# Small VectorE operations split or moved to other forms, transposes planned at their traced length, last feed-forward slots given earlier due numbers

## The chip, the cores and the metric

One core of one Trainium2 chip. The time is the device time of the whole kernel in microseconds: the median of several runs. The engines are named as in the profile: PE (TensorE matmul), PEld (TensorE weight load), DVE (VectorE), ACT (ScalarE), POOL (GpSimd), SP (the queue that issues most DMAs).

## The reference, cut to what matters

```python
# q, k, v: (4, 8, 576, 64); x below: 2304 tokens of 512
scores = q @ k.T / 8
kth    = 32nd largest of each row
attn   = softmax(where(scores >= kth, scores, -1e9)) @ v
h = x @ w_in                                  # 512 -> 2048
x = where(h > 0, h, exp(min(h, 0)) - 1) @ w_out   # 2048 -> 512
logits = normed(x) @ normed(expert_emb).T / tau   # 8 experts
e, gate = argmax(logits), softmax(logits)[e]
out = gate * (relu(x @ w1[e]) @ w2[e])        # 512 -> 1024 -> 512
```

## The kernel before, in words

The kernel has two stages. The first computes attention, the feed-forward layer and the routing, token slot by token slot; the second runs the eight experts on the tokens gathered for each.

Attention works on 144 tiles, each 128 query rows by 576 keys. Two tiles (the two heads of a pair) share one score buffer in SBUF (`arena`), one mask buffer and one transpose. `tile_ops` (from line 760) makes a tile's steps and `threshold` (line 663) its search for the 32nd largest score: PE computes the scores in two halves (L783), ACT copies them to SBUF (L789), VectorE takes the best eight of seven pieces (L677) and from these the best 24 (L687, L689), then a threshold (L691), ACT takes signs against it (L692), VectorE masks the row (L705; in the first 20 tiles POOL does, L703), appends a nine-column filler (L707), finds the next eight (L709) and the final bound (L710). Line 698 makes the exponent's bias from the row maximum, once for each pair of tiles, as three columns read sixteen apart, of which two are used. After that ACT makes a mask (L808), POOL subtracts it (L816), ACT takes the exponential (L818), POOL splits it into two f16 parts (L821, L825), SP transposes these by DMA (L827), and PE multiplies by v (L857). After every eighth tile VectorE counts for a proof that the threshold was right (L715, L716, 8 tiles each).

Keys are fetched by `get_k` (line 533): transposed on PE into the PSUM tile `misc`, of which there is one buffer, and cut into three bf16 parts. For the first 512 columns `thirds` (line 521) does that with ACT copies (L524) and PE matmuls that subtract in PSUM (L526). For the last 64 columns VectorE subtracts (L569, L571) between two ACT copies (L568, L570). Values are cut in two f16 parts by `get_v`: ACT the first (L593), VectorE the second (L597), one instruction for each head.

When the tiles of a slot of 128 tokens are done, `norm_ops` scales the sum (L889), splits it (L894, L895) and transposes it by DMA (L904). `ffn_ops` (line 908) runs the feed-forward layer of the slot in four units of 512 hidden columns: PE (L916 to L918) into the one buffer `hp`, ACT (L938, L939), VectorE (L940), ACT or POOL (L945, L943), POOL (L946), PE (L923 to L925) into `y`. There are 18 slots, counted from 0. `route_ops` (line 957) copies `y` (L962), computes the eight logits of each token (L970, L999), the best expert and its one-hot row (L1000 to L1003), the rank of the token in its expert (L974, L975, L1007, L1008), and the gate (L1006). After slot 14, `first_tokens` gathers 128 tokens of expert 0 (L1026, L1027).

The order on every engine is fixed when the kernel is built. Each step is handed to a planner with an engine, a cost in ns and a due number; the planner (`Plan.emit`, line 149) walks through planned time and starts, of the steps that are ready on an engine, the one with the smallest due number. Due numbers count tiles: a step due at `n` belongs beside tile `n`. Engines then execute their lists in order; a step that waits holds up all behind it on its engine. The costs are numbers in the code: 62 for line 698, 480 for line 1003, 2000 or 1360 for the transposes on SP.

Of the kernel before, what the change touches and what calls it, by code (L numbers as in the profile page):

```python
# [24 lines left out]
BLK = 8  # L25
# [164 lines left out]
def topk_attention_ffn_experts_kernel(  # L190
# [156 lines left out]
    def attention_and_ffn(fast):  # L347
# [185 lines left out]
        def get_k(b, p, due):  # L533
# [15 lines left out]
            def trl():  # L549
                nc.tensor.transpose(m2.t[:, 0:SL], x.t[1].rearrange("p h d -> p (h d)"), ident[0:64, 0:64])  # L550
# [207 lines left out]
        pair, all_s, all_h = {}, [], []  # L758

        def tile_ops(n):  # L760
# [30 lines left out]
            if fast:  # L791
                both = threshold(n, sb, sb.t, top, k, kb, h, sc, halves)
# [700 lines left out]
```

## Time and profile before

| | |
|---|---|
| median of 3 runs | 1298.32 us (1296.48 to 1306.35) |
| profiled execution | 1295.57 us |
| its span, first to last instruction | 1293.7 us |
| busy share of the span | PE 80%, PEld 61%, DVE 71%, ACT 65%, POOL 60% |
| mean granted clock of TensorE | 0.899 of full |

A busy share is an average over both stages. The windows split the span by time; the groups give the mean duration of each instruction of one line and form; a timeline row gives start and duration. An instruction's duration is from its start to its end on the engine; short ones overlap the next by up to some 0.07 us. A duration includes the time in which the engine stands inside the instruction, unable to go on.

### The profile page before, as it was taken

How to read it: one execution, taken by the hardware profiler on the slowest of the kernel's cores; microseconds unless marked ns; L12 is line 12 of the kernel's file. 1: busy time of each engine (PE TensorE's matmuls, PEld its weight loads, DVE VectorE, ACT ScalarE, POOL GpSimd, SP SyncE). 2: the span in 40 equal slices, each digit the busy share in tenths (PEclk: the TensorE clock that was granted, in tenths of full speed). 3: DMA queues.
4: the chain of work that ended last, by engine and by line, in shares of the span. 5: the costliest groups of instructions: out<-in, count | busy, mean ns of one | idle time of the engine just before them, and what ended most of it. 6: DMA issues, size and time to landing. Idle time of an engine off the chain costs nothing. (4 is left out here: it accounts for less than half of the span.)

```text
span 1293.7 us, 28474 instructions
## 1 busy us (share of the span) xinstructions
PE 1037.9 (80%) x10047; PEld 795.6 (61%) x10048; DVE 922.7 (71%) x3597; ACT 846.7 (65%) x1791; POOL 777.0 (60%) x816
## 2 busy tenths in 40 slices
PE   3465446899778899898889978898897779998996
PEld 2344335677556676666566656676664568887885
DVE  4889999798889899999988978998411345334410
ACT  3577768788777788887778958887531345444421
POOL 2258679787778788678878758897622233333300
PEclk9666666899799999899999979998988889999998
DMA  7985642556873558845475655553523555555400
GB/s 207 298 221 141 169 113 50 110 95 142 162 135 61 111 103 150 176 86 99 90 133 101 136 117 103 106 87 68 140 53 91 197 179 180 184 180 167 148 18 17
DMA packets 321732, 165.85 MB, mean 128 GB/s; under 512 B 257990, under 2 KB 298054, under 8 KB 321552
## 3 DMA queue, kind: packets, MB, share of 16 engines
q1 hardware_dynamic: 316816, 150.67, 51.6%
q0 software_dynamic: 4736, 12.92, 3.3%
q8 instruction: 95, 1.56, 0.5%
q14 instruction: 85, 0.70, 0.2%
HBM read 77.43 MB, written 11.40 MB: 69 GB/s over the span
## 5 line engine op out<-in xcount | busy, mean ns | idle before, releaser
L916 PE MATMUL hp<-xt,ww 128*128 128x128 f16 x1152 | 218.2, 230 | 21.3 <-DVE rr L940 20.5
L816 POOL TENSOR_TENSOR arena<-arena,k 128x576 f32<-128x576 f32 x144 | 189.2, 1316 | 76.1 <-ACT k L808 73.7
L917 PE MATMUL hp<-xt,ww 128*128 128x128 f16 x1152 | 217.9, 229 | 0.0
L918 PE MATMUL hp<-xt,ww 128*128 128x128 f16 x1152 | 217.5, 229 | 0.0
L825 POOL TENSOR_TENSOR php<-arena,php 128x576 f16<-128x576 f32 x144 | 187.3, 1301 | 5.8
L783 PE MATMUL sc<-arena_r,qd 128*128 128x288 bf16 (+1 forms) x960 | 149.5, 315 | 50.4 <-DMA arena_r<-big 18.7
L677 DVE MAX8 cand<-arena 128x8 f32<-128x82 f32 (+1 forms) x1008 | 160.9, 228 | 32.1 <-ACT arena L789 31.6
L789 ACT ACTIVATE arena<-sc 128x288 f32<-128x288 f32 x288 | 112.6, 406 | 76.6 <-PE sc L783 72.9
L857 PEld LDWEIGHTS <-pt 128*128 128x128 f16 (+3 forms) x2400 | 100.7, 105 | 99.0 <-DMA pt<-php 55.6
L783 PEld LDWEIGHTS <-qd 128*128 128x128 bf16 (+1 forms) x960 | 87.5, 108 | 96.0 <-issue 37.3
L857 PE MATMUL acc<-vb,pt 128*128 128x64 f16 (+1 forms) x1920 | 93.1, 202 | 56.7 <-DMA pt<-php 44.9
L916 PEld LDWEIGHTS <-ww 128*128 128x128 f16 x1152 | 119.7, 104 | 25.2 <-DVE rr L940 13.8
L821 POOL TENSOR_SCALAR php<-arena 128x576 f16<-128x576 f32 x144 | 101.6, 706 | 55.7 <-ACT arena L818 54.4
L692 ACT ACTIVATE k<-arena,mba 128x576 bf16<-128x576 f32 x144 | 111.6, 775 | 32.0 <-DVE mba L691 26.1
L917 PEld LDWEIGHTS <-ww 128*128 128x128 f16 x1152 | 119.2, 103 | 17.9 <-issue 11.8
L808 ACT ACTIVATE k<-arena,mba 128x576 bf16<-128x576 f32 x144 | 111.7, 775 | 19.3 <-DVE mba L710 14.2
L918 PEld LDWEIGHTS <-ww 128*128 128x128 f16 x1152 | 119.5, 104 | 0.0
L818 ACT ACTIVATE arena<-arena,mx 128x576 f32<-128x576 f32 x144 | 111.5, 775 | 11.4 <-POOL arena L816 9.4
L925 PE MATMUL y<-ww,gt 128*128 128x512 f16 x288 | 111.0, 385 | 3.1 <-POOL gt L946 3.1
L923 PE MATMUL y<-ww,gt 128*128 128x512 f16 x288 | 112.0, 389 | 1.6 <-ACT big L962 1.0
L709 DVE MAX8 w<-w 128x8 f32<-128x585 f32 x144 | 109.8, 762 | 4.0 <-POOL w L703 2.9
L924 PE MATMUL y<-ww,gt 128*128 128x512 f16 x288 | 111.2, 386 | 0.0
(303 smaller groups left out, 2774.9 us busy)
## 6 DMA issues: line engine op xcount, KB each, us to landing
arena<-in_moe_w_dram SPq DMA_DIRECT2D x52, 512.0 KB
arena_r<-big SPq DMA_DIRECT2D x64, 144.0 KB
big<-in_moe_w_out_dram SPq DMA_DIRECT2D x16, 512.0 KB
ww<-in_moe_w_in_dram SPq DMA_DIRECT2D x14, 512.0 KB
qd<-big SPq DMA_DIRECT2D x32, 192.0 KB
ysc<-big SPq DMA_DIRECT2D x20, 258.0 KB
w<-in_moe_w_dram SPq DMA_DIRECT2D x10, 512.0 KB
big<-in_v_dram SPq DMA_DIRECT2D x9, 512.0 KB
```

Source lines behind the costliest of these rows:

```text
L677: v.max(out=cand.t[:, 8 * g:8 * g + 8], in_=x()[:, ENDS[g]:ENDS[g + 1]])
L692: op("act", 760, n + K["dsg"], lambda: nc.scalar.activation(k.t(), x(), AF.Sign, scale=-1.0, bias=th.t, accum_out=ds.t), r=[sb, th, k.base ...
L783: nc.tensor.matmul(o[64 * g:64 * g + 64] if s is None else o, qd.t[:, i, g, p * n:p * n + n], kt.t[:, g, i // 2, cs], start=i == 0, stop=i ...
L789: op("act", 291, n - K["dcp"], lambda c=c: nc.scalar.activation(sb.t()[:, c * 288:c * 288 + 288], sc.t[:, SC0 + c * 288:SC0 + c * 288 + 28 ...
L808: op("act", 667, n + K["drl"], lambda: nc.scalar.activation(k.t(), sb.t(), AF.Relu, scale=-HUGE, bias=kb.t), r=[sb, kb, s2, k2], w=[k])
L816: op("pool", 1242, e, lambda sb_=sb_, k_=k_: nc.gpsimd.tensor_tensor(sb_.t(), sb_.t(), k_.t(), op=ALU.subtract), r=[k_, s2, k2], w=[sb_])
L825: op("pool", 1270, e + K["dlo"], lambda sb_=sb_, i=i: nc.gpsimd.tensor_tensor(ph.t[:, i, 1, 0:S], sb_.t(), ph.t[:, i, 0, 0:S], op=ALU.subt ...
L857: nc.tensor.matmul(acc.t[out_, cs], t[h][rows, g, :], rhs, start=(i == 0), stop=(i == len(units) - 1))
L916: nc.tensor.matmul(hp.t[:, i * 128:i * 128 + 128], wi_at(0, kb, fb), xh, start=(kb == 0), stop=False)
L917: nc.tensor.matmul(hp.t[:, i * 128:i * 128 + 128], wi_at(0, kb, fb), xl, start=False, stop=False)
L918: nc.tensor.matmul(hp.t[:, i * 128:i * 128 + 128], wi_at(1, kb, fb), xh, start=False, stop=(kb == KB - 1))
L923: nc.tensor.matmul(y.t, gt.t[:, 0, i, :], wo_at(0, fb), start=(fb == 0), stop=False)
```

## The change

The diff makes these edits (lines of the kernel before):

1. The bias of the exponential (L698): instead of one instruction of three columns for each pair of tiles, one of a single column for each tile (144 instead of 64 with three columns and 16 with one).
2. The last 64 columns of a key block go through `thirds` like the first 512: three ACT copies from PSUM and two PE matmuls, and no VectorE step.
3. The second part of the values (L597): one VectorE instruction for both heads.
4. The proof counts (L715, L716) are made after every 16th tile.
5. Routing: the logits are written to a spare part of `misc` in PSUM and read from there by L1000, L1001 and ACT's L1006; the rank sum (L1007) goes to PSUM too and is read there by L1008. The one-hot row (L1003) is written as nine columns, three by three, from a new constant `rev9`, whose rows of three are four apart.
6. The planner's cost of the transpose on SP: 3100 and 1900 instead of 2000 and 1360. Other costs follow edits 1 to 5.
7. The last four feed-forward slots (14, 15, 16, 17) get due numbers 1, 2, 3 and 4 tiles earlier at their first unit and twice as much earlier at their end.

```diff
-BLK = 8
+BLK = 16
...
+    rev9 = const.tile([128, 3, 4], F32, name="rev9")
+    for i in range(9):
+        nc.vector.memset(rev9[:, i // 3, i % 3:i % 3 + 1], float(E - i))
...
-            mx = None
-            if h or tiles[n][3] is None:
-
-                mx = r_mx()
-                op("dve", 62, n + .3, lambda: v.tensor_scalar(mx.t[:, 0:2 * h + 1], top.t[:, 0:32 * h + 1:16], -scale, None, op0=ALU.mult), r=[top], w=[mx])
+            if not h:
+                pair["mx"] = r_mx()
+            mx2, mx = pair["mx"], Buf(t=1)
+            op("dve", 62, n + .3, lambda: v.tensor_scalar(mx2.t[:, h:h + 1], place(0)[:, 0:1], -scale, None, op0=ALU.mult), r=[top, mx2], w=[mx])
...
-            left = r_left()
-            end = piece(SM, SL)
-            op("act", 110, due - U, lambda: nc.scalar.activation(end(0), m2.t[:, 0:SL], AF.Copy), r=[m2, kn], w=[kx2])
-            op("dve", 130, due - U, lambda: nc.vector.tensor_tensor(left.t, m2.t[:, 0:SL], end(0), op=ALU.subtract), r=[m2, kn, kx2], w=[left])
-            op("act", 110, due - U, lambda: nc.scalar.activation(end(1), left.t, AF.Copy), r=[left, kn], w=[kx2])
-            op("dve", 130, due - U, lambda: nc.vector.tensor_tensor(end(2), left.t, end(1), op=ALU.subtract), r=[left, kn], w=[kx2])
+            thirds(kx2, m2, SL, due - U, piece(SM, SL), 110, [kn])
...
-                for hd in range(2):
-                    op("dve", 700 if i == 0 else 300, due, lambda i=i, hd=hd: lo(i, hd), r=[x, b_sv], w=[d])
+                op("dve", 950 if i == 0 else 400, due, lambda i=i: lo(i), r=[x, b_sv], w=[d])
...
-            op("sp", 2000 if nh == 2 else 1360, e + .6, lambda: nc.sync.dma_start_transpose(
+            op("sp", 3100 if nh == 2 else 1900, e + .6, lambda: nc.sync.dma_start_transpose(
...
+            def LG():
+                return m2.t[:, 3 * E:4 * E]
...
-            op("dve", 380, e, lambda: v.scalar_tensor_tensor(X(1)[:, 2], X(1)[:, 0], X(1)[:, 1, 0:1], rev8, op0=ALU.is_equal, op1=ALU.mult), r=[x, lgt, mx], w=[er])
+            op("dve", 130, e, lambda: v.scalar_tensor_tensor(X(1)[:, 2], LG(), X(1)[:, 1, 0:1], rev8, op0=ALU.is_equal, op1=ALU.mult), r=[x, m2, lgt, mx], w=[er])
...
-            op("dve", 480, e, lambda: v.tensor_scalar(X(2), rev8, X(1)[:, 3, 0:1], None, op0=ALU.is_equal), r=[x, er], w=[one_])
+            op("dve", 130, e, lambda: v.tensor_scalar(
+                X(2).rearrange("p (a b) -> p a b", a=3), rev9[:, :, 0:3], X(1)[:, 3, 0:1], None, op0=ALU.is_equal), r=[x, er], w=[one_])
...
-            op("act", 290, e, lambda: nc.scalar.activation(X(1)[:, 4], X(1)[:, 0], AF.Exp, bias=X(0)[:, 2:3], accum_out=X(0)[:, 3:4]), r=[x, lgt, ng], w=[pr])
+            op("act", 290, e, lambda: nc.scalar.activation(X(1)[:, 4], LG(), AF.Exp, bias=X(0)[:, 2:3], accum_out=X(0)[:, 3:4]), r=[x, m2, lgt, ng], w=[pr])
...
-                ffn_ops(where[b, j], e, e + K["ffd"])
+
+                c = max(0, where[b, j] - NSLOT + 5)
+                ffn_ops(where[b, j], e - c, e - c + K["ffd"] - c)
```

What that does to the order, at three places. The line numbers of the changed kernel differ: between 680 and 810 they are one or two lower (its 686, 690, 696, 703, 705, 707, 708, 713, 714, 787 and 806 are 687, 691, 698, 705, 707, 709, 710, 715, 716, 789 and 808 of before), its 527 is 524 (and 568, 570), its 591 is 593, its 1001 to 1006 are 998 to 1003, its 1011 to 1016 are 1007 to 1012; from 818 to 962 they are the same.

VectorE at the threshold of the last tile, before:

```order
2096 L687 MAX top<-cand 128x8
2097 L691 TENSOR_SCALAR mba<-top 128x1
2098 L698 TENSOR_SCALAR mx<-top 128x3
2099 L705 SCALAR_TENSOR_TENSOR w<-sc,mba,arena 128x576
2100 L707 TENSOR_SCALAR w<-ramp,dsa 128x9
2101 L709 MAX w_14209<-w 128x8
2102 L710 TENSOR_SCALAR mba<-w_14209 128x1
2103 L715 TENSOR_TENSOR ge<-w_14209,mba 128x64
```

and now:

```order
2120 L686 MAX top<-cand 128x8
2121 L690 TENSOR_SCALAR mba<-top 128x1
2122 L696 TENSOR_SCALAR mx<-top 128x1
2123 L703 SCALAR_TENSOR_TENSOR w<-sc,mba,arena 128x576
2124 L705 TENSOR_SCALAR w<-ramp,dsa 128x9
2125 L707 MAX w_13445<-w 128x8
2126 L708 TENSOR_SCALAR mba<-w_13445 128x1
2127 L713 TENSOR_TENSOR ge<-w_13445,mba 128x128
2128 L714 TENSOR_REDUCE cnta<-ge 128x16
```

The three-column instruction is now one of a single column, and the count covers sixteen tiles.

VectorE from the scaling of the last slot (L889) on, with the feed-forward step L940 (one for each unit) and the routing of slot 16, before:

```order
2125 L889 TENSOR_TENSOR rr<-acc,rinv 128x512
2126 L1012 RECIPROCAL big<-ss 128x1
2127 L1007 TENSOR_TENSOR L<-misc,bcap 128x8
2128 L1008 SCALAR_TENSOR_TENSOR L,ss<-L,oh 128x8
2129 L1010 TENSOR_TENSOR bcap<-misc,bcap 128x8
2130 L940 SCALAR_TENSOR_TENSOR rr<-hp,sc_115,rr 128x512 x3
2131 L998 RECIPROCAL ss<-ss 128x1
2132 L999 TENSOR_SCALAR L<-misc,ss,taub 128x8
2133 L1000 MAX L<-L 128x8
2134 L1001 SCALAR_TENSOR_TENSOR L<-L,rev_81 128x8
2135 L1002 MAX L<-L 128x8
2136 L1003 TENSOR_SCALAR oh<-rev_81,L 128x8
```

and now:

```order
2154 L889 TENSOR_TENSOR rr<-acc,rinv 128x512
2155 L1001 RECIPROCAL ss<-ss 128x1
2156 L1002 TENSOR_SCALAR misc<-misc,ss,taub 128x8
2157 L1003 MAX L<-misc 128x8
2158 L1004 SCALAR_TENSOR_TENSOR L<-misc,L,rev_81 128x8
2159 L1005 MAX L<-L 128x8
2160 L1006 TENSOR_SCALAR oh<-rev_83,L 128x9
2161 L1011 TENSOR_TENSOR misc<-misc,bcap 128x8
2162 L1012 SCALAR_TENSOR_TENSOR L,ss<-misc,oh 128x8
2163 L1014 TENSOR_TENSOR bcap<-misc,bcap 128x8
2164 L1016 RECIPROCAL big<-ss 128x1
2165 L940 SCALAR_TENSOR_TENSOR rr<-hp,sc_125,rr 128x512 x4
```

Before, two units of slot 16 stood behind L889 (in the x3, with one of slot 17); now all four of slot 17 and none of slot 16, and slot 16's routing is finished ahead of slot 17's first unit.

ACT at the third key block of the second batch, whose last 64 columns are the rows with 128x64, before:

```order
622 L524 ACTIVATE big<-misc 128x512
623 L593 ACTIVATE vb<-vraw,sv 128x8x64
624 L789 ACTIVATE arena<-sc 128x288
625 L568 ACTIVATE big<-misc 128x64
626 L808 ACTIVATE k<-arena,mba 128x576
627 L789 ACTIVATE arena<-sc 128x288
628 L570 ACTIVATE big<-left 128x64
```

and now:

```order
636 L527 ACTIVATE big<-misc 128x512
637 L939 ACTIVATE rr<-rr,sc_125 128x512
638 L591 ACTIVATE vbl<-vrawl,sv 64x2x64
639 L527 ACTIVATE big<-misc 128x64
640 L806 ACTIVATE k<-arena,mba 128x576
641 L787 ACTIVATE arena<-sc 128x288
642 L527 ACTIVATE big<-misc 128x64
643 L787 ACTIVATE arena<-sc 128x288 x3
644 L527 ACTIVATE big<-misc 128x64
```

There are three copies out of `misc` instead of one out of `misc` and one out of `left`, with other steps of ACT between them.

## Rows read from the trace of the kernel before

**Rows 1.** Windows: length, busy PE, PEld, DVE, ACT, POOL, clock, DMA share, GB/s.

```profile
0.00:100.00 100.00, 47.99 (x308) 33.95 (x310) 68.21 (x259) 58.58 (x125) 32.46 (x35) 0.72 0.86 242
...
100.00:200.00 100.00, 45.69 (x435) 35.09 (x434) 98.33 (x299) 72.56 (x137) 74.67 (x54) 0.62 0.50 131
...
200.00:900.00 700.00, 605.91 (x6956) 448.52 (x6957) 626.93 (x2777) 564.63 (x1277) 545.73 (x608) 0.94 0.59 111
```

**Rows 2.** VectorE instruction groups by form: total busy, mean ns, idle before.

```profile
L709 DVE MAX8 w<-w 128x8 f32<-128x585 f32 x144 | 109.8, 762 | 4.0 <-POOL w L703 2.9
...
L687 DVE MAX8 top<-cand 128x8 f32<-128x56 f32 x432 | 85.2, 209 | 2.4
...
L698 DVE TENSOR_SCALAR mx<-top 128x3 f32<-128x3 f32 x64 | 44.8, 699 | 0.0
...
L707 DVE TENSOR_SCALAR w<-ramp,dsa 128x9 f32<-128x9 f32 x144 | 30.5, 212 | 10.6 <-ACT k L692 10.0
...
L597 DVE SCALAR_TENSOR_TENSOR vb<-vraw,sv,vb 128x256 f16<-128x256 f32 x32 | 24.3, 759 | 2.0 <-ACT vb L593 1.9
...
L691 DVE TENSOR_SCALAR mba<-top 128x1 f32<-128x1 f32 x144 | 20.9, 145 | 1.4
...
L597 DVE SCALAR_TENSOR_TENSOR vbl<-vrawl,sv,vbl 64x64 f16<-64x64 f32 x32 | 18.8, 588 | 2.5 <-ACT vbl L593 2.5
...
L571 DVE TENSOR_TENSOR big<-left,big 128x64 bf16<-128x64 f32 x16 | 13.1, 816 | 2.7 <-ACT big L570 2.6
...
L715 DVE TENSOR_TENSOR ge<-w,mba 128x64 f32<-128x64 f32 x18 | 12.8, 713 | 0.0
...
L1003 DVE TENSOR_SCALAR oh<-rev,L 128x8 bf16<-128x8 f32 x18 | 9.8, 542 | 0.1
...
L1001 DVE SCALAR_TENSOR_TENSOR L<-L,rev 128x8 f32<-128x8 f32 x18 | 9.3, 514 | 0.1
...
L569 DVE TENSOR_TENSOR left<-misc,big 128x64 f32<-128x64 f32 x15 | 3.2, 214 | 1.1 <-ACT big L568 0.9
...
L698 DVE TENSOR_SCALAR mx<-top 128x1 f32<-128x1 f32 x16 | 2.3, 143 | 0.0
```

**Rows 3.** Lines 698 and 707 by themselves: duration min/median/max in ns.

```profile
L698 DVE TENSOR_SCALAR mx<-top x80: 139/206/4152, 23.4 to 907.5; 128x3 f32<-128x3 f32 x64, 128x1 f32<-128x1 f32 x16
...
L707 DVE TENSOR_SCALAR w<-ramp,dsa x144: 175/211/224, 24.5 to 912.3; 128x9 f32<-128x9 f32 x144
```

**Rows 4.** Lines 698, 597, 571 in turn: VectorE busy within 200 to 900.

```profile
200.00:900.00 700.00, 39.47 (x70) 0.94 0.59 111
...
200.00:900.00 700.00, 29.30 (x48) 0.94 0.59 111
...
200.00:900.00 700.00, 11.08 (x12) 0.94 0.59 111
```

**Rows 5.** TensorE waits: total us, times, longest.

```profile
PE misc L526 <- ACT big L524: 21.6, 24, 3.6
```

**Rows 6.** Timeline from 907 to 976 on POOL, DVE, SP and ACT.

```profile
907.46 4.15 DVE L698 TENSOR_SCALAR mx<-top 128x3 f32<-128x3 f32 x1
...
915.45 1.01 POOL L1027 DMA_INDIRECT big<-ysc,ids  x1 [3.87 <-DMA ids<-lst]
...
932.88 0.69 DVE L889 TENSOR_TENSOR rr<-acc,rinv 128x512 f32<-128x512 f32 x1 [0.70 <-PE acc L857]
...
935.50 1.23 SPq L904 DMA_TRANSPOSE xt<-xs  x1
...
948.14 0.69 ACT L962 ACTIVATE big<-y,sc 128x512 f32<-128x512 f32 x1 [4.90 <-PE y L925]
...
958.70 0.69 ACT L938 ACTIVATE rr<-hp,sc 128x512 f32<-128x512 f32 x1 [2.60 <-PE misc L975]
...
969.23 0.69 ACT L938 ACTIVATE rr<-hp,sc 128x512 f32<-128x512 f32 x1 [2.29 <-PE hp L918]
...
975.93 0.69 ACT L962 ACTIVATE big<-y,sc 128x512 f32<-128x512 f32 x1 [3.66 <-PE y L925]
```

More of the change, by code (lines that the diff above doesn't have):

```diff
@@ L549, in trl @@
             def trl():
-                nc.tensor.transpose(m2.t[:, 0:SL], x.t[1].rearrange("p h d -> p (h d)"), ident[0:64, 0:64])
+                turned(m2.t[:, 0:SL], x.t[1].rearrange("p h d -> p (h d)"), 64, 0)
             def piece(a, n):
@@ L593, in hi, with lo @@
                 nc.scalar.activation(h, src, AF.Copy, scale=sv[:src.shape[0], 0:1])
-            def lo(i, hd):
+            def lo(i):
                 src, h, l = parts(i)
-                nc.vector.scalar_tensor_tensor(l[:, hd], src[:, hd], sv[:src.shape[0], 0:1], h[:, hd], op0=ALU.mult, op1=ALU.subtract)
+                if not i:
+                    src, h, l = src.rearrange("p h r d -> p (h r) d"), d.t[0].rearrange("p h r x d -> p (h r) x d")[:, :, 0, :], d.t[0].rearrange("p h r x d -> p (h r) x d")[:, :, 1, :]
+                nc.vector.scalar_tensor_tensor(l, src, sv[:src.shape[0], 0:1], h, op0=ALU.mult, op1=ALU.subtract)
             op("sp", 1100, due - 2, load, w=[x], lat=DLAT, after=hold)
@@ L659, in attention_and_ffn @@
         sums, pts, accs, xts = {}, {}, {}, {}
-        proofs, block = [], {}
+        proofs, block, pair = [], {}, {}
         def threshold(n, sb, x, top, k, kb, h, sc, halves):
@@ L714, in threshold @@
                 ths = mba[:, n0:n0 + BLK, 1:2].to_broadcast([128, BLK, 8])
-                op("dve", 560, n + 4, lambda: v.tensor_tensor(ge.t, w8b.t, ths, op=ALU.is_ge), r=block["own"] + [w8b], w=[ge])
+                op("dve", 900, n + 4, lambda: v.tensor_tensor(ge.t, w8b.t, ths, op=ALU.is_ge), r=block["own"] + [w8b], w=[ge])
                 op("dve", 135, n + 5, lambda: v.tensor_reduce(cnta[:, n0:n0 + BLK], ge.t, op=ALU.add, axis=AX.X), r=[ge], w=[cn])
@@ L756, in __new__ @@
                 return b
-        pair, all_s, all_h = {}, [], []
+        all_s, all_h = [], []
         def tile_ops(n):
@@ L791, in tile_ops @@
             if fast:
-                both = threshold(n, sb, sb.t, top, k, kb, h, sc, halves)
+                mb = threshold(n, sb, sb.t, top, k, kb, h, sc, halves)
             else:
@@ L811, in tile_ops @@
                 return
-            heads = [(a, k_, x, both if fast else x, i_) for a, k_, x, i_ in ([pair["first"]] if s else []) + [(sb, k, mb, i)]]
+            heads = ([pair["first"]] if s else []) + [(sb, k, mb, i)]
             nh, e = len(heads), n + K["de"]
-            for i, (sb_, k_, mb_, by, i_) in enumerate(heads):
-                mx_ = (lambda i=i: both.t[:, 2 * i:2 * i + 1]) if fast else (lambda mb_=mb_: mb_.t)
+            mx2 = pair["mx"] if fast else None
+            for i, (sb_, k_, mb_, i_) in enumerate(heads):
+                mx_ = (lambda i=i: mx2.t[:, i:i + 1]) if fast else (lambda mb_=mb_: mb_.t)
+                by = [mb_, mx2] if fast else [mb_]
                 op("pool", 1242, e, lambda sb_=sb_, k_=k_: nc.gpsimd.tensor_tensor(sb_.t(), sb_.t(), k_.t(), op=ALU.subtract),
@@ L818, in tile_ops @@
                 op("act", 760, e + K["dex"], lambda sb_=sb_, mx_=mx_, i_=i_: nc.scalar.activation(
-                    sb_.t(), sb_.t(), AF.Exp, scale=scale, bias=mx_(), accum_out=sm_.t[:, i_:i_ + 1]), r=[by, s2], w=[sb_, sm_])
+                    sb_.t(), sb_.t(), AF.Exp, scale=scale, bias=mx_(), accum_out=sm_.t[:, i_:i_ + 1]), r=by + [s2], w=[sb_, sm_])
                 if fast:
@@ L1002, in route_ops @@
+            op("dve", 77, e, lambda: v.max(out=X(1)[:, 1], in_=LG()), r=[x, m2, lgt], w=[mx])
+            op("dve", 130, e, lambda: v.scalar_tensor_tensor(X(1)[:, 2], LG(), X(1)[:, 1, 0:1], rev8, op0=ALU.is_equal, op1=ALU.mult), r=[x, m2, lgt, mx], w=[er])
             op("dve", 77, e, lambda: v.max(out=X(1)[:, 3], in_=X(1)[:, 2]), r=[x], w=[er])
-            op("dve", 480, e, lambda: v.tensor_scalar(X(2), rev8, X(1)[:, 3, 0:1], None, op0=ALU.is_equal), r=[x, er], w=[one_])
+            op("dve", 130, e, lambda: v.tensor_scalar(
+                X(2).rearrange("p (a b) -> p a b", a=3), rev9[:, :, 0:3], X(1)[:, 3, 0:1], None, op0=ALU.is_equal), r=[x, er], w=[one_])
```

14 lines of the change are left out of this document (6 added, 8 removed).

## The prediction

> **What bounds the kernel now.** I read the windows first [rows 1]. From 200 to 900 us, where attention and feed-forward run side by side, VectorE is busy 626.9 of 700 us (89.6%), ACT 564.6 (80.7%), POOL 545.7 (78%), PE 605.9 (87%, with pipelined ends counted, so less than it looks). From 100 to 200 us VectorE is busy 98.33 of 100. From 0 to 100 it is busy 68% while the DMA engines are at 0.86: that stretch waits for loads. So VectorE sets the pace from 100 to 900, and the 318 us after 976 (of the span's 1293.7) belong to the experts, which the change does not touch.
>
> Then the VectorE groups by form [rows 2]. The reader is to see how odd the means are. One column costs 145 ns (L691), nine columns read three by three cost 212 (L707), but three columns cost 699 (L698), eight cost 542 and 514 (L1003, L1001), and 64 columns from two SBUF tensors cost 816 (L571). Size does not explain it. The spread does [rows 3]: L698 takes 139 ns at best, 206 in the middle and 4152 at worst, L707 never more than 224. L698 is an operation that at times stands still inside its own duration, and L707 is not. The waits do not show this, since the engine counts as busy.
>
> **The change part by part,** in VectorE time, first whole, then from 200 to 900.
>
> Bias (L698): 44.8 + 2.3 = 47.1 us in 80 instructions [rows 2]. Now 144 of one column at 0.145 (the mean of L691, same form): 20.9. Saved 26. From 200 to 900 there are 39.5 us in 70 instructions [rows 4]; they become 126, 18.3 us: 21.2 saved. After 900 one instruction is left, at 907.46, for the last tile; its 4.15 us [rows 6] become 0.3: 3 to 4 us.
>
> Values (L597): 24.3 + 18.8 = 43.1 in 64 instructions. A column costs (762 - 209) / (585 - 56) = 1.05 ns by L709 and L687. So 16 at 759 + 268 = 1027 ns and 16 at 588 + 67 = 655 ns: 26.9. Bounds: 16 x (759 + 588) = 21.6 if width were free, 43.1 if it doubled all. They still read two SBUF tensors and may still stand. Saved 16, of which 29.3 x (1 - 26.9 / 43.1) = 11.0 from 200 to 900 [rows 4] and 5.2 before, between 100 and 200.
>
> Keys (L569, L571): 3.2 and 13.1 go whole; 12 of the 16 fetches are in the stretch, 11.1 us of L571 [rows 4] and 12 x 0.214 = 2.6 of L569: 13.7. The four others lie in the first 100 us and are worth nothing there. The price is one more ACT copy of 64 columns a fetch; its like is not in the rows, between 0.15 (one column on VectorE) and 0.69 (512 columns on ACT, [rows 6]); at 0.25, 3 us of ACT in the stretch. It adds two PE matmuls a fetch, each waiting for an ACT copy. PE waits 0.9 us (21.6 over 24) for the existing ones [rows 5]. Behind such a matmul stand scores and feed-forward on PE. The order gives ACT other work between the copies, so I count 0 to 3 us on the path, and take 1.
>
> Counts (L715): 18 x 713 ns become 9 x (713 + 67): 12.8 to 7.0, 5.8 saved, 4.9 in the stretch. I leave the small reduction behind it out.
>
> Routing: L1003 takes the form of L707, 18 x 0.212 = 3.8 instead of 9.8. L1001 reads one operand from PSUM; nearest is again L707, 3.8 instead of 9.3 (bounds 18 x 0.145 = 2.6 and no gain). L1008 I count as no gain. Saved 11.5, of which 15/18, 9.6, in the stretch. ACT's L1006 now waits for the rank matmuls on PE, since both touch `misc`; behind it on ACT stand masks and exponentials, but the plan puts it after them and its result goes only to the slot's store. I cost this, and the longer hold of `misc`, at 1 us; without that cover each of 18 routings could cost one PE wait of 0.9.
>
> A rule that speaks against the last form: by the Trainium skill, "VectorE: DVE Perf Modes", section "What auto-detection actually checks", a one-source SBUF operation takes both ports when the outermost dimensions of source and target are equal, and three rows of three would be such; by the same skill's "SBUF — State Buffer", section "SBUF: two separate sides", that is what makes VectorE and GpSimd block one another. L707 has just this form, three by three, and never stood in 144 instructions (at most 224 ns, [rows 3]), so the trace disagrees and the row decides. By the rule L1003 would keep its 9.8 us, and the forecast would be 4 us higher.
>
> In all from 200 to 900: 21.2 + 11.0 + 13.7 + 4.9 + 9.6 = 60.4, so VectorE falls from 626.9 to 566.5. ACT rises from 564.6 to 567.6. Now two engines are equal, and each feeds the other: scores go ACT, VectorE, ACT, POOL, ACT, POOL. What share can they hold? VectorE alone holds 89.6% now with ACT at 80.7%. I take 86.5%, since two level engines make each other wait: 567 / 0.865 = 655, 45 saved. At 89.6% it would be 633 (the whole 60 saved); at 83%, 683, 17 saved. From 100 to 200 VectorE has no slack and the 5.2 + 0.8 of values and bias pass whole: 6.
>
> Transposes: on SP a longer planned cost moves PE's value matmuls behind other work. That costs nothing by itself, and I count no gain.
>
> Last slots. Slot 17's scaling starts at 932.88 and its transpose is issued at 935.50 and done issuing at 936.73, but slot 16's `y` is copied only at 948.14, and slot 17's second unit reaches ACT at 958.70 [rows 6]. From the second to the fourth unit, 969.23 - 958.70 = 10.53, a unit takes 5.27; from the fourth to the copy 975.93 it takes 6.70. In the new order two units of slot 16 have moved ahead of L889, and slot 16's routing stands ahead of slot 17's units. If slot 17 starts when its transpose lands (936.7 to 940), its end is half a unit (2.6), three units (15.8) and 6.7 later: 962 to 965. With a routing of slot 16 still in between, some 2 more. Saved 9 to 12; less if the units moved ahead delay the last tiles on PE: 4 to 12, I take 9. POOL's gather (L1027) moves ahead too, past several of the last subtractions; its wait of 3.87 for the list [rows 6] falls earlier, behind it the subtractions of four tiles instead of one. POOL has slack there; I count nothing. Expert weights on SP keep their place behind the last transposes.
>
> Sum: 6 + 45 + 3 + 9 saved, 2 added: 61. The profiled execution has 1295.6 (its span and 1.9 around it); 1234.6. The runs shown have a median 2.7 above it: **1237**.
>
> **Rivals.** (a) ACT becomes the bound early. For it: it is at 80.7% already, and the search goes through it five times a tile. Against: its idle time is mostly waiting for others. At 83%: 6 + 17 + 3 + 9 = 35 saved, 1295.6 - 35 + 2.7 = 1263.
>
> (b) The standing time was cover for other waits. Whatever VectorE loses, it then spends waiting for ACT's copies. Only the tail's 9 is gained, perhaps 3 at the start: 1286. Against: 98% from 100 to 200, and the means differ so much in one form that the plan (62 ns for L698, 699 measured) cannot have covered it.
>
> (c) Slower: `misc` has one buffer. 16 key fetches hold it for two more trips from PE to ACT, 18 routings until ACT's L1006. At PE's 0.9 us a trip that is 32 x 0.9 + 18 x 0.9 = 45 us of PE standing in order. If PE set the pace, VectorE's savings would be worth nothing: 1295.6 + 45 - 9 + 2.7 = 1334. It decides once PE is busy above some 95% from 200 to 900; it is at 87%, and the order puts work between the trips.
>
> (d) All of it passes: 6 + 60 + 4 + 12 = 82 saved, 1216.
>
> **How the numbers follow.** The forecast, 1220 to 1255, and what lies around it up to 1262: 0.56. (d) and below: 0.05. (a): 0.20. (b): 0.12. (c): 0.07. The range that leaves out no more than 2 in 10 takes in (d) and (a) and ends short of (b): 1210 to 1284. Faster by over 1% (below 1285; about what a measurement of this kernel can tell from no change) holds the forecast, (d) and (a): 0.81. Within 1%: 0.12. Slower: 0.07.
>
> **What would show it.** In the changed kernel's profile: L698's successor at 145 ns with no instruction above 0.3 us, L1003's at 212, L1001's near 0.2, L597's at 1.03 and 0.66. VectorE's busy time from the first tile to the last some 75 us less. ACT's share above VectorE's or level with it. Slot 17's first unit on PE right after its transpose lands, and 31 to 34 us, not 43, from its L889 to its `y` copy. It would be wrong if VectorE's idle time grew by what its busy time lost (b), if PE's waits before L526's successor passed 40 us (c), or if the one-column operations also stood still.

## The result, and the profile after

The changed kernel takes 1251.8 us (median of 6 runs, 1250.0 to 1258.9) where the kernel before takes 1300.9 (6 runs, 1296.4 to 1307.4): 49 us less by the medians. The ratio on record is 0.9648, 95% interval 0.9608 to 0.9688, which is 3.5% or 46 us. The forecast was 1237 in a range of 1210 to 1284, from a sum of 61 us. The profiled execution shown here took 1257.4, 38 less than the 1295.6 of the one before.

The windows, to be held against [rows 1] (length, busy PE, PEld, DVE, ACT, POOL with instruction counts, clock, DMA share, GB/s); 865 is where the last search ends:

```profile
0.00:100.00 100.00, 55.21 (x382) 41.07 (x383) 70.78 (x270) 63.73 (x137) 38.83 (x39) 0.85 0.87 244
100.00:200.00 100.00, 50.97 (x495) 38.72 (x492) 99.27 (x322) 77.91 (x146) 82.14 (x59) 0.66 0.56 135
200.00:865.00 665.00, 600.33 (x7082) 445.28 (x7083) 576.13 (x2775) 564.97 (x1293) 546.27 (x611) 0.95 0.61 118
```

VectorE is busy in 86.6% of the 665 us (576.13), ACT in 85%, PE in 90%. The forecast was a stretch of 655 us and a share of 86.5%. The VectorE groups by form answer to [rows 2] (busy, mean ns | idle before):

```profile
L705 DVE TENSOR_SCALAR w<-ramp,dsa 128x9 f32<-128x9 f32 x144 | 31.0, 215 | 26.9 <-ACT k L691 25.7
L696 DVE TENSOR_SCALAR mx<-top 128x1 f32<-128x1 f32 x144 | 20.6, 143 | 0.0
L597 DVE SCALAR_TENSOR_TENSOR vb<-vraw,sv,vb 128x512 f16<-128x512 f32 x16 | 18.0, 1123 | 1.3 <-ACT vb L591 1.1
L597 DVE SCALAR_TENSOR_TENSOR vbl<-vrawl,sv,vbl 64x128 f16<-64x128 f32 x16 | 11.5, 721 | 0.1
L713 DVE TENSOR_TENSOR ge<-w,mba 128x128 f32<-128x128 f32 x9 | 6.8, 752 | 0.0
L1004 DVE SCALAR_TENSOR_TENSOR L<-misc,L,rev 128x8 f32<-128x8 f32 x18 | 4.0, 222 | 0.1
L1006 DVE TENSOR_SCALAR oh<-rev,L 128x9 bf16<-128x9 f32 x18 | 4.0, 220 | 0.1
```

L696 is L698's successor, L705 is L707's, L1004 and L1006 are those of L1001 and L1003. The bias went from 47.1 to 20.6 us, and its 144 instructions take 131, 144 and 151 ns at least, in the middle and at most: nothing of the 4152 is left.

The timeline of the tail (DVE, then ACT, then DVE and ACT again), against [rows 6]:

```profile
863.76 0.77 DVE L707 MAX8 w<-w 128x8 f32<-128x585 f32 x1
...
887.51 0.69 ACT L938 ACTIVATE rr<-hp,sc 128x512 f32<-128x512 f32 x1 [2.86 <-PE hp L918]
...
892.16 0.69 DVE L889 TENSOR_TENSOR rr<-acc,rinv 128x512 f32<-128x512 f32 x1 [2.33 <-PE acc L857]
...
904.89 0.69 ACT L938 ACTIVATE rr<-hp,sc 128x512 f32<-128x512 f32 x1 [0.63 <-PE hp L918]
...
929.06 0.69 ACT L962 ACTIVATE big<-y,sc 128x512 f32<-128x512 f32 x1 [3.66 <-PE y L925]
```

The last of the 144 long searches (L707, before L709) starts at 863.76 instead of 912.50: 48.7 earlier. From there to slot 17's `y` copy it is 65.3 us, before 63.4 (975.93 - 912.50). The copy waits for the same work in both (`y`, L925), and slot 17's scaling L889 now comes 28.4 us behind the last search, before 20.4. The experts' stage behind the copy was 317.8 us and is 326.5 in this execution, though its code is the same; the other kernels below lie between 317 and 326. With the medians 49 apart, I read the 38 of the two profiled executions mostly as their scatter. The eight kernels whose copy comes before 940 us have 323.5 there in the mean and the six others 320.0, so this stage may also give a few us back; why it varies stays open.

What the sum did not contain is seen in the waits. Kernel before, 200 to 800 us, TensorE, then VectorE (total us, times, longest):

```profile
PE acc L857 <- DMA pt<-php: 35.1, 17, 4.0
...
DVE cand L677 <- ACT arena L789: 17.9, 17, 3.3
...
DVE w L707 <- ACT k L692: 8.1, 15, 1.2
```

Changed kernel, same stretch:

```profile
DVE w L705 <- ACT k L691: 23.2, 31, 3.1
PE acc L857 <- DMA pt<-php: 20.9, 16, 4.0
...
DVE cand L676 <- ACT arena L787: 10.4, 18, 1.4
```

L857 is the value matmul on PE; it waits for the transposed exponentials `pt`. The wait fell by 14 us, and VectorE's search L676 waits less for ACT's copies. By `e3` and `e6` below both come with edit 6, to which the prediction gave nothing. VectorE's wait at L705 for ACT's signs (L691; L707 and L692 before) went the other way, from 8.1 to 23.2, so VectorE spends part of what it saved in waiting.

### The profile page after: what moved, and what is told of

Read it like the earlier page. It is cut to its first block, busy times and chain, and to the rows that moved or that the text cites. A ratio compares the mean times of both kernels' runs of the same rounds, so it can differ in the third digit from the quotient of the medians.

```text
span 1255.6 us, 28591 instructions
## 1 busy us (share of the span) xinstructions
PE 1036.1 (83%) x10112; PEld 799.0 (64%) x10112; DVE 865.1 (69%) x3588; ACT 847.8 (68%) x1807; POOL 780.8 (62%) x816
## 5 line engine op out<-in xcount | busy, mean ns | idle before, releaser
L781 PE MATMUL sc<-arena_r,qd 128*128 128x288 bf16 (+1 forms) x960 | 145.5, 308 | 43.2 <-ACT arena L787 17.7
L676 DVE MAX8 cand<-arena 128x8 f32<-128x82 f32 (+1 forms) x1008 | 161.3, 229 | 26.1 <-ACT arena L787 25.2
L857 PEld LDWEIGHTS <-pt 128*128 128x128 f16 (+3 forms) x2400 | 99.7, 104 | 68.6 <-DMA pt<-php 36.3
L916 PEld LDWEIGHTS <-ww 128*128 128x128 f16 x1152 | 119.8, 104 | 27.1 <-DVE rr L940 15.3
L691 ACT ACTIVATE k<-arena,mba 128x576 bf16<-128x576 f32 x144 | 111.4, 774 | 14.8 <-DVE mx L696 7.7
L857 PE MATMUL acc<-vb,pt 128*128 128x64 f16 (+1 forms) x1920 | 91.5, 201 | 32.7 <-DMA pt<-php 30.8
L925 PE MATMUL y<-ww,gt 128*128 128x512 f16 x288 | 109.2, 379 | 4.6 <-POOL gt L946 4.6
L707 DVE MAX8 w<-w 128x8 f32<-128x585 f32 x144 | 109.9, 763 | 4.1 <-POOL w L701 3.2
L923 PE MATMUL y<-ww,gt 128*128 128x512 f16 x288 | 109.5, 380 | 0.6 <-ACT gt L945 0.6
L924 PE MATMUL y<-ww,gt 128*128 128x512 f16 x288 | 109.1, 379 | 0.0
```

The costliest lines, as they stand in the source:

```text
L676: v.max(out=cand.t[:, 8 * g:8 * g + 8], in_=x()[:, ENDS[g]:ENDS[g + 1]])
L691: op("act", 760, n + K["dsg"], lambda: nc.scalar.activation(k.t(), x(), AF.Sign, scale=-1.0, bias=th.t, accum_out=ds.t), r=[sb, th, k.base ...
L781: nc.tensor.matmul(o[64 * g:64 * g + 64] if s is None else o, qd.t[:, i, g, p * n:p * n + n], kt.t[:, g, i // 2, cs], start=i == 0, stop=i ...
L857: nc.tensor.matmul(acc.t[out_, cs], t[h][rows, g, :], rhs, start=(i == 0), stop=(i == len(units) - 1))
L916: nc.tensor.matmul(hp.t[:, i * 128:i * 128 + 128], wi_at(0, kb, fb), xh, start=(kb == 0), stop=False)
```

## Experiments

**Parts alone and parts left out.** Theory from the prediction: VectorE's standing time is what passes. Rivals: the plan's costs carry the gain, or VectorE's quicker work only turns into waits.

Bias alone (`e1`), put into the kernel before:

```diff
-... v.tensor_scalar(mx.t[:, 0:2 * h + 1], top.t[:, 0:32 * h + 1:16], ...
+... v.tensor_scalar(mx2.t[:, h:h + 1], place(0)[:, 0:1], ...
```

> The kernel before with the bias of the exponentials alone made one column per tile (edit 1). Theory (VectorE's small operations stand still inside their own duration while GpSimd works, and that time sits on the path): the new groups of 144 one-column operations have a mean near 0.145 us and a longest below 0.3; VectorE's busy time falls by 25 us; the end comes 18 to 24 us earlier (ratio 0.981 to 0.986), of which 3 to 4 in the last tile's bias. Rival (the standing was cover, and the gain of the whole change came from planned costs and order): within 5 us of before. Rival (a VectorE that is quicker only waits for ACT): below 8 us.

Measured: 1283.1 us, 0.9899 (0.9869 to 0.9929), 13 us faster. The group falls to 143 ns as expected; the gain lies between the two theories.

All but the bias (`e2`), the three columns put back into the changed kernel:

```diff
-... v.tensor_scalar(mx2.t[:, h:h + 1], place(0)[:, 0:1], ...
+... v.tensor_scalar(mx.t[:, 0:2 * h + 1], top.t[:, 0:32 * h + 1:16], ...
```

> The changed kernel with the bias put back to three columns for two heads (all edits but 1). Theory: the three-column groups stand again, mean near 0.7 us with single ones of 2 us and more; the time lies 18 to 26 us above the changed kernel, 25 to 32 us below the kernel before. Rival (the bias carries nearly all of it): 40 us above the changed kernel or more. Rival (the bias carries nothing): within 5 us of the changed kernel.

Measured: 1265.3 us, 0.976 (0.9724 to 0.9796). Against the whole change's 0.9648 that is 1.1%, 14 us, less than the 18 expected. By itself or on top of the rest, the bias is worth 13 to 14. The three-column group stands again (46.3 us, mean 724 ns), but the plan shifted too: PE's wait for `pt` from 200 to 800 us is 9.9 us here and 20.9 in the changed kernel, which is the faster one.

Transposes' planned cost alone (`e3`), in the kernel before:

```diff
-op("sp", 2000 if nh == 2 else 1360, ...
+op("sp", 3100 if nh == 2 else 1900, ...
```

> The kernel before with the planned cost of the transposes alone raised to 3100 and 1900 (edit 6). Theory: it costs and gains nothing, within 4 us of before; PE's wait for `pt` (44.9 us over the profiled execution of the kernel before) shrinks, and other waits of PE grow by as much. Rival (the better plan is where the gain comes from): 10 to 25 us earlier than before.

Measured: 1276.6 us, 0.9856 (0.982 to 0.9891), 19 us faster. My theory fell here: two numbers of the plan, which change no instruction's work, bring as much as the bias or more. Its waits on TensorE, 200 to 800:

```profile
PE sc L783 <- DVE w L705: 20.6, 20, 3.5
PE acc L857 <- DMA pt<-php: 16.9, 13, 4.0
```

The wait for `pt` is 16.9 us instead of 35.1, and PE's wait for VectorE's masks (L705) grew from 12.7 to 20.6. So a part came back as another wait, where I had expected all of it to. VectorE's busy time in this stretch rose from 534.5 to 545.2, with no instruction of it quicker: so it had not been full.

Without the last slots (`e4`), the changed kernel less edit 7:

```diff
-c = max(0, where[b, j] - NSLOT + 5)
-ffn_ops(where[b, j], e - c, e - c + K["ffd"] - c)
+ffn_ops(where[b, j], e, e + K["ffd"])
```

> The changed kernel with the last slots due as in the kernel before (all edits but 7). Theory from the two traces (moving two units of slot 16 ahead only moved the last value matmuls behind them): within 3 us of the changed kernel; slot 17's scaling L889 some 20 us after the last search, and 42 to 43 us from there to its `y` copy. The prediction's own tail term: 9 us slower than the changed kernel.

Measured: 1248.1 us, 0.96 (0.9562 to 0.9638), against 0.9648 (0.9608 to 0.9688) with edit 7: no difference that these intervals show, and not 9 us slower. L889 starts 24.1 us behind the last search (expected 20), and the `y` copy 38.9 behind L889 (expected 42 to 43); both together 63.0 instead of 65.3.

**A new theory: PE's order.** PE works through its list in the planned order. A value matmul planned before its transpose has landed makes PE stand, with scores behind it; ACT's copies of these scores come late, and so does VectorE's search. The first test leaves SP's planned cost as before and raises only the latency behind the transpose (`e5`):

```diff
-... r=[ph], w=[pt], lat=DLAT)
+... r=[ph], w=[pt], lat=DLAT + (1100 if nh == 2 else 540))
```

> The kernel before, with the transposes' cost on SP left as it was and their planned latency raised by the same 1100 and 540: value matmuls are planned later on PE, while SP's own plan is not filled by longer transposes. Theory (edit 6 gains because value matmuls no longer stand in PE's order ahead of data that has not landed, with scores behind them): 12 to 22 us earlier than before, PE's wait for `pt` from 200 to 800 us falls from 35.1 to 25 us or less. Rival (the gain lies in SP's changed order of loads and transposes): within 5 us of before.

Measured: 1280.3 us, 0.9884 (0.9839 to 0.993), 15 us faster, with this TensorE wait, so the gain does not need SP's longer occupation:

```profile
PE acc L857 <- DMA pt<-php: 15.3, 11, 4.2
```

All that VectorE does otherwise, without the plan (`e6`, edits 1 to 5; these lines of the changed kernel as in the kernel before):

```diff
-op("sp", 3100 if nh == 2 else 1900, ...
-ffn_ops(where[b, j], e - c, e - c + K["ffd"] - c)
+op("sp", 2000 if nh == 2 else 1360, ...
+ffn_ops(where[b, j], e, e + K["ffd"])
```

> The kernel before with edits 1 to 5 (all that VectorE does otherwise), without the transposes' cost and the last slots. As the prediction reckoned (VectorE's saved time passes at three quarters): 45 to 52 us earlier than before. By the two runs in hand (bias alone 13, transposes' cost alone 19, the whole 46 to 49): 25 to 34 us earlier. If edits 2 to 5 bring nothing of their own: 10 to 16 us earlier, as the bias alone.

Measured: 1286.0 us, 0.9922 (0.9891 to 0.9953), 10 us faster: the last case, no more than the bias alone. The window (length, then busy PE, PEld, DVE, ACT, POOL), and the waits of TensorE, VectorE and ACT, 200 to 800:

```profile
200.00:800.00 600.00, 524.42 (x6051) 382.17 (x6050) 496.56 (x2380) 490.31 (x1124) 469.64 (x521) 0.94 0.63 117
...
PE acc L857 <- DMA pt<-php: 39.7, 23, 4.1
...
DVE cand L676 <- ACT arena L787: 31.1, 26, 7.1
DVE w L705 <- ACT k L691: 28.6, 28, 3.6
...
ACT arena L787 <- PE sc L781: 53.8, 42, 7.5
```

VectorE's busy time is 496.6 us in 600, 37.9 less than before, and nearly all of it has become idle: PE stands 39.7 at the value matmuls, ACT waits 53.8 for scores, VectorE 31.1 for ACT's copies and 28.6 for ACT's signs. This is the prediction's rival (b), for edits 1 to 5 by themselves. Beside `e3` and `e4` it makes a square: edits 1 to 5 bring 0.8%, edit 6 brings 1.4%, both together 4.0%, that is 1.8% (23 us) more than the two apart, and the three intervals together leave some 0.6% either way.

**More of the same.** If a wait of PE costs its length, the remaining 20.9 us can go as well. Two ways, both in the changed kernel: a still longer planned cost on SP (`e9`, 4200 and 2600), and 1100 more latency (`e10`):

```diff
-op("sp", 3100 if nh == 2 else 1900, ...
+op("sp", 4200 if nh == 2 else 2600, ...
```

```diff
-... r=[ph], w=[pt], lat=DLAT)
+... r=[ph], w=[pt], lat=DLAT + 1100)
```

> The changed kernel with the transposes' planned cost raised once more, to 4200 and 2600. Theory (edit 6 gains because the planned cost now meets the traced one: an issue takes 3.1 us in the median and lands after 5.0, planned are 3100 and 2100 behind it): a further rise gains nothing; within 5 us of the changed kernel, up to 10 slower, since the plan now holds SP's loads back for transposes that have long ended. Rival (the longer the better, as PE still waits 20.9 us for `pt` from 200 to 800): 5 to 12 us earlier, with that wait halved.

> The changed kernel with 1100 more planned latency behind each transpose (SP's own cost as in the changed kernel). PE's wait for `pt` from 200 to 800 us falls from 20.9 to 12 or less in either case. Theory (the plan already meets the traced landing): within 5 us of the changed kernel. Rival (any wait of PE for `pt` still costs its length in time): 5 to 12 us earlier.

Measured: `e9` 1248.8 us, 0.9627 (0.958 to 0.9675), no change that shows; `e10` 1233.3 us, 0.9498 (0.9457 to 0.954), some 19 us faster than the changed kernel and the best of the kernels that leave nothing out. For `e10` the rival is right, though the gain is larger than its 5 to 12 us; for `e9` it is not, although the wait was halved as it asked. TensorE's waits in `e9`, then in `e10`:

```profile
PE acc L857 <- DMA pt<-php: 10.6, 9, 2.4
```

```profile
PE acc L857 <- DMA pt<-php: 4.9, 7, 1.7
```

So 15 to 19 us of time went with 16 to 20 us of this wait in `e3`, `e5` and `e10`, and none that shows went with 10 us of it in `e9`. A longer planned landing also reorders every engine behind it, so that the wait itself costs its length is argued and not shown. A second path is PE's clock: over the same 112 tiles PE's busy time (with modelled ends) is 546.2 us at a mean granted clock of 0.93 of full in the kernel before, 533.9 at 0.94 in the changed one and 529.5 at 0.96 in `e10`. The gain of `e3` came without it (543.7 at 0.93); in the others no run tells the two apart.

In `e9` the 112 tiles of the middle are 8.9 us quicker, and the first 16 and the last 15 are each 5 us slower (table below). That would fit loads held back on SP, which I did not test, but it may be scatter. The starts of the long search number 17, 129 and 144, and of slot 17's `y` copy, in each profiled execution, and the steps between them in us:

| kernel | to 17 | 17 to 129 | 129 to 144 | to the copy | PE's wait for `pt`, 200 to 800 |
|---|---|---|---|---|---|
| before | 197.6 | 635.4 | 79.6 | 63.4 | 35.1 |
| `e1` bias | 197.7 | 620.6 | 73.8 | 66.7 | 34.5 |
| `e2` edits 2 to 7 | 191.7 | 598.0 | 80.5 | 63.8 | 9.9 |
| `e3` plan | 191.3 | 620.5 | 77.1 | 64.1 | 16.9 |
| `e5` latency | 195.9 | 617.7 | 82.2 | 64.1 | 15.3 |
| `e6` edits 1 to 5 | 188.2 | 624.4 | 77.7 | 69.2 | 39.7 |
| `e4` edits 1 to 6 | 185.7 | 604.4 | 70.2 | 63.0 | 22.7 |
| changed | 184.3 | 602.3 | 77.1 | 65.3 | 20.9 |
| `e9` cost more | 189.2 | 593.4 | 81.8 | 60.4 | 10.6 |
| `e10` latency more | 185.2 | 584.2 | 79.9 | 63.8 | 4.9 |
| `e11` value first | 183.9 | 598.9 | 78.2 | 64.4 | 19.3 |
| `e12` latency, no edit 7 | 186.1 | 582.8 | 77.5 | 69.1 | 5.3 |

Each row is one execution, and the times of one kernel lie 7 to 19 us apart, so only the large steps count. `e2` shows it: its profiled execution took 1257.1, the shortest of its six, and the changed kernel's 1257.4, near its longest.

**The tail.** Value matmuls of the last tile first (`e11`):

```diff
-op("pe", 985, n + K["dav"], av, ...
+op("pe", 985, n + (1.5 if n == N - 1 else K["dav"]), av, ...
```

> The changed kernel with the value matmuls of the last tile due two tiles earlier, so that on PE they stand ahead of the last 1.7 units of slot 16's second product and last quarter of its first, which then fill the round trip from slot 17's scaling to its transposed input. Theory from the traces (in the changed kernel the moved units stand between the last search and slot 17's scaling): slot 17's scaling 20 to 23 us behind the last search instead of 28.4, its `y` copy 60 to 62 us behind the last search instead of 65.3; 3 to 6 us earlier than the changed kernel. Rival (PE is full to the end whatever the order): within 2 us.

Measured: 1246.5 us, 0.9605 (0.9559 to 0.9651), not to be told from the changed kernel. VectorE's timeline (a time and a length in us):

```profile
882.60 0.69 DVE L889 TENSOR_TENSOR rr<-acc,rinv 128x512 f32<-128x512 f32 x1 [0.16 <-POOL ss L1015]
```

L889 starts 21.6 us behind the last search (861.00), as planned, but the `y` copy comes 64.4 behind it (925.39), not 60 to 62: the rival's case. And the best kernel without edit 7 (`e12`, against `e10`):

```diff
-ffn_ops(where[b, j], e - c, e - c + K["ffd"] - c)
+ffn_ops(where[b, j], e, e + K["ffd"])
```

> The kernel of the run with 1100 more latency, now with the last slots due as in the kernel before (edits 1 to 6 and the latency, without edit 7). Theory from the tails in hand (63.0 us from the last search to slot 17's `y` copy without edit 7, 65.3, 64.4 and 63.8 with it in three kernels: the order of these units only moves waits): within 4 us of the run with edit 7, 1230 to 1237. If edit 7 pays once value matmuls are planned at their landing: 5 to 10 us slower. If it costs: 4 to 8 us faster. In all cases below both the kernel before and the changed one; PE's wait for `pt` from 200 to 800 us at 8 or less.

Measured: 1238.4 us, 0.954 (0.9503 to 0.9578) against 0.9498 (0.9457 to 0.954): the intervals overlap, so edit 7 has no worth that these runs show, in either plan. My theory (1230 to 1237) missed all the same: the median is 5 us slower, at the lower edge of the case in which edit 7 pays, and the `y` copy comes 69.1 us behind the last search instead of 63.8. `e4` points the other way by 4 us, so whether edit 7 pays in the better plan stays open.

**What holds the middle now.** A third of the first product's matmuls left out (`e8`; the end of the sum moves to the second of the three):

```diff
-nc.tensor.matmul(..., wi_at(1, kb, fb), xh, start=False, stop=(kb == KB - 1))
```

> The changed kernel without the third matmul of each group in the first feed-forward product (the weights' low part, L918, 1152 matmuls of 228 ns, is left out, so the output is less exact); the plan is the same. It asks what holds the pace of the middle stretch in the changed kernel, 602 us for 112 tiles with PE busy 90% and VectorE 87%. If PE (rival to the prediction's picture): 30 us or more off these 602, and VectorE's share rises above 91%. If VectorE, ACT and POOL with their mutual waits: less than 12 us off.

Measured: 1224.2 us (one run). The 112 tiles take 583.4 instead of 602.3 us, 19 less, between the two cases. The 228 ns of the expectation are the length of one matmul up to its modelled end, and do not say what the engine gives up without it. In the changed kernel's timeline of PE the next one starts 0.05 to 0.06 us behind it (0.056 in the mean over such a run):

```profile
500.67 0.22 PE L916 MATMUL hp<-xt,ww 128*128 128x128 f16 x1
500.73 0.22 PE L917 MATMUL hp<-xt,ww 128*128 128x128 f16 x1
500.78 0.22 PE L918 MATMUL hp<-xt,ww 128*128 128x128 f16 x1
```

By this spacing the matmuls left out are worth an estimated 50 us in 112 of the 144 tiles (1152 x 112 / 144 x 0.056), and PE's busy time over these tiles fell by 41, from 533.9 to 493.3. So 4 to 5 in 10 of what PE does less passes: PE alone does not hold the pace, and it has a large part in it.

**Which forms stand still** (`e7`): one extra VectorE operation per tile, eight forms in turn on lines 701 to 709 (three of them here):

```diff
+lambda: v.tensor_scalar(pb.t[:, 0:3], top.t[:, o:o + 24:8], 2.0, None, op0=ALU.mult),
...
+lambda: v.tensor_tensor(pb.t[:, 0:8], top.t[:, o:o + 8], top.t[:, o + 8:o + 16], op=ALU.add),
+lambda: v.tensor_scalar(pb.t[:, 0:8], sc.t[:, SC0:SC0 + 8], 2.0, None, op0=ALU.mult),
```

> The changed kernel with one small extra VectorE operation per tile behind the bias, its form turning through eight lines (18 instructions each); its result goes unused. Theory (an operation stands still when it reads or writes SBUF in a form other than the one-column and the three-by-three one, with GpSimd at work 80% of the time): one column, three by three and eight columns out of PSUM have a longest below 0.35 us; three columns, eight columns and the one- and eight-column operations with two SBUF sources have means of 0.35 us or more with a longest above 1 us; two columns is open (means of 0.15 or of 0.4 and more). Rival (what decides is having two SBUF sources, and three columns stood for another reason): eight and three columns stay below 0.35. Rival (the place in the program decides, not the form): all eight have like means.

Measured, the instructions that write the extra tile (duration in ns, least/median/most):

```profile
L701 DVE TENSOR_SCALAR pb<-top x18: 143/145/149, 22.0 to 819.6; 128x1 f32<-128x1 f32 x18
L702 DVE TENSOR_SCALAR pb<-top x18: 157/590/3118, 57.7 to 830.2; 128x2 f32<-128x2 f32 x18
L703 DVE TENSOR_SCALAR pb<-top x18: 151/224/3189, 75.9 to 838.3; 128x3 f32<-128x3 f32 x18
L704 DVE TENSOR_SCALAR pb<-top x18: 152/236/1084, 95.3 to 849.8; 128x8 f32<-128x8 f32 x18
L705 DVE TENSOR_SCALAR pb<-top x18: 150/153/155, 111.0 to 862.6; 128x9 f32<-128x9 f32 x18
L707 DVE TENSOR_TENSOR pb<-top x18: 146/405/1160, 135.1 to 876.3; 128x1 f32<-128x1 f32 x18
L708 DVE TENSOR_TENSOR pb<-top x18: 152/450/6051, 158.9 to 887.5; 128x8 f32<-128x8 f32 x18
L709 DVE TENSOR_SCALAR pb<-sc x18: 151/156/159, 178.0 to 897.6; 128x8 f32<-128x8 f32 x18
```

One column, three by three (L705) and eight columns out of PSUM (L709) never stand. Two, three and eight plain columns of one SBUF source do, and so does a single column with two SBUF sources. At their best all eight take 143 to 157 ns, so it is the form and not the size or the place. Both rivals fall. GpSimd's timeline shows where a stand ends: of the 48 of these 144 instructions that took more than 0.3 us, all started while a GpSimd instruction ran, and 45 ended within 0.05 us of the end of one; of L698's 80 in the kernel before, 37 took more than 0.3 us, and all of them ended so. No run took GpSimd's work away. The longest case on VectorE's timeline, and GpSimd's beside it:

```profile
620.45 6.05 DVE L708 TENSOR_TENSOR pb<-top 128x8 f32<-128x8 f32 x1
626.43 0.81 DVE L718 SCALAR_TENSOR_TENSOR w<-sc,mba,arena 128x576 f32<-128x576 f32 x1
...
620.35 1.29 POOL L831 TENSOR_TENSOR arena<-arena,k 128x576 f32<-128x576 f32 x1
621.59 1.29 POOL L840 TENSOR_TENSOR php<-arena,php 128x576 f16<-128x576 f32 x1
622.82 1.16 POOL L961 TENSOR_TENSOR gt<-rr,gt 128x512 f16<-128x512 f32 x1
623.94 1.30 POOL L836 TENSOR_SCALAR php<-arena 128x576 f16<-128x576 f32 x2
625.22 1.26 POOL L840 TENSOR_TENSOR php<-arena,php 128x576 f16<-128x576 f32 x1
```

It stands from 620.45 until 626.50, through six GpSimd instructions without a gap, and ends with the last of them at 626.48. The eight forms take 71 us of VectorE in all; the kernel took 1279.4 (one run), 28 more than the changed kernel's median. So, by this one run, about 4 in 10 of what VectorE does more pass in the changed kernel, much as with PE's work in `e8`: neither engine holds the middle alone.

The Trainium skill, "SBUF — State Buffer", section "SBUF: two separate sides", says that an operation with two SBUF inputs needs the port pair that VectorE shares with GpSimd (against a GpSimd operation that reads SBUF), and that whoever starts first has it for the whole instruction. The trace agrees on who stands (one column with two sources: up to 1160 ns), and shows more than one instruction's wait: 6.05 us where a GpSimd instruction takes 1.3.

## Why the prediction was right in sum and wrong in its shares

- **Bounds.** "So VectorE sets the pace from 100 to 900" was the first step that failed. Its share was highest, but taking 37.9 of 600 us from it alone (`e6`) brought 10 us in all. PE's stands at value matmuls (35.1 us from 200 to 800; [rows 5] shows only another wait of PE) were not weighed. `e3`, `e5` and `e10` show that the plan around them is worth 15 to 19 us, while by `e7` and `e8` VectorE's and PE's own work each pass at about 4 in 10.
- **Transposes.** The step "costs nothing by itself, and I count no gain" failed: 19 us alone (`e3`), and it is what lets edits 1 to 5 pass. A sign of it lay in the trace before: SP's issue of a transpose, planned at 2.0 us, takes 3.1 in the median (first fence: least/median/most), and in the changed kernel it lands 5.0 us after its issue in the median (second, a row of its DMA view), where 2000 + 2100 ns were planned before and 3100 + 2100 now. That a further 1100 still paid (`e10`) suggests that the median was not the right aim.

```profile
L827 SPq DMA_TRANSPOSE pt<-php x80: 1282/3114/5791, 38.1 to 926.1; - x80
```

```profile
pt<-php SPq DMA_TRANSPOSE x80, 5.0
```

- **Sizes on VectorE.** Bias, counts and routing came as worked out (143, 752, 222 and 220 ns; forecast 145, 780, 212 and 212). Values were under-sized: 1123 and 721 ns instead of 1027 and 655, so 13.6 us saved and not 16; they still read two SBUF tensors and still stand (up to 2269 ns). VectorE's busy time fell by 57.6 us over the whole execution (922.7 to 865.1) and not by some 75; part of that is that the busy time counts overlaps once and the groups' sums do not. The rule as the prediction read it, by which the three-by-three form would stand, is not borne out by L1006 (at most 228 ns) or by the 155 ns above.
- **What passes, 45 + 6 + 3.** The last search came 48.7 us earlier, forecast 54 less 2. The share assumed, 86.5%, was measured as 86.6%, and that is luck: it was set by judgement. It holds for edits 1 to 6 together; for edits 1 to 5 it is 82.8% (496.6 of 600). The size was right because a gain that I had left out made up for a loss that I had put down to a rival. One bound was wrong in itself: 700 to 633 us is 67 saved and not 60, so rival (d) should have been 1209 and not 1216.
- **Tail, 9.** Mis-sized: the tail grew by 1.9 us. L889 to the copy did shrink from 43.1 to 36.9 (forecast 31 to 34), but L889 comes 8.0 us later after the last search. About half of that came without edit 7: it is 24.1 to 24.6 us in `e1`, `e4` and `e6`, 20.4 before. Edit 7 itself put the last value matmuls behind slot 16's units on PE, which `e11` undid (21.6). From `e4` to the changed kernel it added 4.3 us ahead of L889 and took 2.0 behind it. By `e4` and `e11` the order of these units moves the wait and not the end; `e12` leaves that open for the better plan.
- **Costs, 2.** PE's wait for the key ends' copies did not grow (first row below, whole execution: 15.7 us over 19; before 21.6 over 24, [rows 5]), and rival (c) is refuted. The longer hold of `misc`, put at 1 us together with ACT's wait, was mis-sized: VectorE's rank steps now wait for ACT's gate step (L1010, L1006 before), which reads `misc` too. From 100 to 900 us that is 12.6 us (the other three rows; 9.7 in `e6`, nothing in the kernel before), about as much as the 11.5 that edit 5 was to save. What this idle time costs was not tested.

```profile
PE misc L529 <- ACT big L527: 15.7, 19, 3.5
...
DVE misc L1011 <- ACT L L1010: 8.5, 5, 3.5
...
DVE bcap L1014 <- ACT L L1010: 2.6, 3, 1.4
DVE L L1012 <- ACT L L1010: 1.5, 4, 0.6
```

- **Rivals.** (a) came in part: ACT's share is 85%, level with VectorE's, and PE's is above both. (b) is true of edits 1 to 5 alone. (d) did not come. The best kernel, `e10` at 1233.3, lies near the forecast; it needed a step that the forecast did not contain.

## What to carry to other kernels

An engine that is 90% busy need not be the bound where another, working in a fixed order, stands for late data: add up the waits at instructions with long queues behind them (here 35 us at the value matmuls), and test a scheduler's planned costs and latencies against the traced ones (2.0 planned, 3.1 taken) before shortening work. Of the small VectorE operations tried beside a busy GpSimd, those with one SBUF source of one column or of three rows of three, and those with a PSUM source, never stood; a spread of 139 to 4152 ns in one form is the sign to look for. An edit judged by itself (10 us for five edits, 19 for one) says little of the pair (52). A matmul's length in the profile is not its cost: what it takes from PE is the step to the next start (0.056 us here, for a length of 0.22).

## What the runs showed of the hardware that was not expected

- An operation of VectorE stood for 6.05 us through six GpSimd instructions in a row, not only for the one that was running; 82 of the 85 stands of over 0.3 us looked at here (45 of 48 and 37 of 37) ended within 0.05 us of the end of a GpSimd instruction.
- Two columns of one SBUF source stand (median 590, longest 3118 ns), as do eight contiguous ones (longest 1084), while nine as three by three do not (longest 155) and eight out of PSUM do not (longest 159).
- A transpose issue on SP (two heads' 128 x 2560 elements in f16 for most of the 80) takes 3.1 us in the median, from 1.3 to 5.8.
